# Query loads moved ahead, first load behind mu, and output tiles stored by one DMA

## The chip, the cores and the metric

The kernel runs on one core of a Trainium2 chip. The core has five engines that this document names: PE (TensorE, matrix multiplication), DVE (VectorE), ACT (ScalarE), POOL (GpSimd) and SP (SyncE, which here only issues DMAs). Sixteen DMA engines serve the core. DMAs are issued from SP, ACT or POOL; each of the three has its own queue, and all queues share the sixteen DMA engines. The metric is device time of one execution in microseconds (us), as the median of several executions; lower is better.

## The reference

The computation is an attention through 32 memory slots per head, followed by a gated feed-forward layer. Batch 8, 8 heads, 576 positions, head size 64, so 512 features; the hidden layer has 1024.

```python
def _attn_ref(q, k, v, phi):                      # q, k, v: (8, 8, 576, 64); phi: (8, 8, 576, 32)
    a = softmax(phi over the 576 positions)
    k_m = einsum('bhsm,bhsd->bhmd', a, k)         # 32 memory keys per head
    v_m = einsum('bhsm,bhsd->bhmd', a, v)         # 32 memory values per head
    attn = softmax(q @ k_m^T / sqrt(64))          # 576 x 32 per head
    return attn @ v_m

def _moe_ref(x, mu_k, mu_r, w_k, w_v, w_r):       # x: (8, 576, 512), the heads side by side
    x_prev = x shifted by one position, zeros first
    xk = mu_k * x + (1 - mu_k) * x_prev
    xr = mu_r * x + (1 - mu_r) * x_prev
    k = relu(xk @ w_k)
    v = (k * k) @ w_v
    return sigmoid(xr @ w_r) * v                  # (8, 576, 512), float32
```

## The kernel before

Work goes batch by batch. Of a batch, the exponentials of `phi` (tile `em`) are multiplied with `k` and `v` (tile `kv`) into the memory keys and values (`kvps`), the keys are normalised and transposed (`kbd`, `ktps`, `kmT`), the query is transposed on DVE (`qT`, line 384), the scores (`scps`) are exponentiated on ACT and normalised (`atn`). For batches 1 to 7 the memory values are first multiplied into the weights (`G`), so that the hidden layer (`pk`, `rl`, `sq`) and the gate (`pr`, `sg`) come straight from `atn`. Batch 0 goes the direct way, through the mixed input `x0T`. The output of a tile of 128 positions is `pv` = `sq` times `w_v` on PE, multiplied with the gate into a tile `o` of 128 partitions by 512 float32 on DVE (line 751), and stored from there. There are four buffers of `o`, used in turn: the tile after the next three cannot be written before the stores of this one have landed.

The order is written out by hand. `PLAN` is a list of words that a loop at the end of the function walks through; each word emits the instructions of one step, and every engine executes its instructions in that order. `0:kg0` is a step of batch 0's attention, `c0:7a` a block of the hidden layer, `o:73` an output tile (its first mention emits the matmuls, its second the DVE multiplication and the store), `b:3x8` filler matmuls on zeros that keep PE busy, and `p:...` a load. `p:q:0a` and `p:q:0b` are the two parts of batch 0's query: b the last 4 of 9 column blocks (512 KB read), a the first 5 (640 KB read). Words `0:q1` and `0:q0` transpose these two parts; both write and read one query tile, so program order decides which waits for which.

All loads but the first are issued by POOL's queue, in program order, and convert float32 to bf16 on the way (not `phi`). The list `PRE` is emitted ahead of `PLAN`: the word `id` builds the identity matrix on POOL, `after` is a one-element copy on POOL into `mark` that waits for a load and so holds back what POOL issues behind it. `phi` and `k` of batch 0 are issued on ACT's queue at the very start (lines 169 and 178), and `mu_k` and `mu_r` on SP's queue, 2 KB each (lines 181 and 182): four rows of 128 float32.

Stores are issued by SP (line 728), in the three words of `TAIL` alternately by SP and ACT. An output tile of a batch b > 0 holds four groups of 32 positions; group v goes to rows 18u + 8h' + 2v + r of the output (u from 0 to 31), so a tile is stored by four DMAs of 32 rows:

```python
for v in range(4):
    parts.append((out[b].rearrange("(u x) d -> x u d", u=PB)[8 * h + 2 * v + r], v * PB, PB))
```

Tiles `e0` to `e3` collect what is left of two batches each (two or four parts of 32 rows per tile), and batch 0's tiles consist of parts of 32 or 64 rows, stored in two halves of 256 columns.

Of the kernel before, what the change touches and what calls it, by code (L numbers as in the profile page):

```python
# [17 lines left out]

PLAN = [
# [65 lines left out]

WARM = (10, 8)

PRE = "id: after: q:0b"
TAIL = ("o:70", "o:e3a", "o:e3b",)


NJ = 9
# [5 lines left out]
def kernel(  # L98
# [13 lines left out]
    nc = tc.nc  # L112
# [9 lines left out]
    QR = S // NJ  # L122
    PB = QR // 2
# [34 lines left out]
    mark = const.tile([1, 1], F32, name="mark")  # L158
# [3 lines left out]
    loads = {}  # L162

    def rows(src):
        return src.rearrange("h s d -> (h s) d").rearrange("(a p j) d -> p a (j d)", a=HH, j=NJ)

    def load_phi(b, eng):
        ph = ld.tile([128, HH, NJ, M], F32, name="ph", tag="ph")
        eng.dma_start(out=ph.rearrange("p h j m -> p h (j m)"), in_=rows(phi[b]))
        loads[b] = ph  # L170

    def load_rows(dst, src):
        nc.gpsimd.dma_start(out=dst.rearrange("p h j d -> p h (j d)"), in_=rows(src))
# [6 lines left out]
    mu2 = const.tile([2 * ND, 128], F32, name="mu2")  # L180
# [13 lines left out]
    def preload(word):  # L194

        what, _, part = word.partition(":")
        if what in weights:
            dst, src = weights[what]
            f0, f1 = (int(x) * 128 for x in part.split("-"))
            nc.gpsimd.dma_start(out=dst[:, :, f0:f1], in_=src[:, :, f0:f1])  # L200
        elif what == "id":
            make_identity(nc, identity)
        elif what == "after":
            nc.gpsimd.tensor_copy(mark, loads[0][:1, 0, 0, :1])
        else:
            n = int(part[0])
            if what == "phi":
                load_phi(n, nc.gpsimd)
            else:
                dst = qs[n % 2].rearrange("p (h j) d -> p h j d", j=NJ) if what == "q" else kvs[n % 2][:, "kv".index(what)]  # L210
                src = {"q": q, "k": k, "v": v}[what][n]
                if part[1:] in ("a", "b"):
                    js = HALVES["ab".index(part[1])]
                    js = slice(js.start // QR, js.stop // QR)
                    nc.gpsimd.dma_start(out=dst[:, :, js].rearrange("p h j d -> p h (j d)"),
                                        in_=rows(src)[:, :, js.start * D:js.stop * D])
                elif part[1:] in ("g", "h"):
                    gs = slice(0, 2) if part[1] == "g" else slice(2, 4)
                    nc.gpsimd.dma_start(out=dst[:, gs].rearrange("p h j d -> p h (j d)"), in_=rows(src)[:, gs])
                else:  # L220
                    load_rows(dst, src)

    for word in PRE.split():
        preload(word)
# [12 lines left out]
    for g in range(4):  # L237
        r = slice(g * M, (g + 1) * M)
# [11 lines left out]
    def keep_busy(n, blocks=CT // 64):  # L250
        ps = ps_tile([128, CT], F32, "idle", cover=blocks * 64)[:, :blocks * 64]
        for _ in range(n):
            nc.tensor.matmul(ps.rearrange("p (a b) -> p a b", b=64), lhsT=zeros,  # L253
                             rhs=zeros[:, :64].unsqueeze(1).to_broadcast([128, blocks, 64]), start=True, stop=True,
                             skip_group_check=True)
# [390 lines left out]
    TILES = (0, 128, NP, NP + 128)  # L646
# [56 lines left out]
    queues = [nc.sync]  # L703

    def store(name, o, cols):
        parts = []
        if name[0] == "e":
            for x, b in enumerate((2 * int(name[1]), 2 * int(name[1]) + 1)):
                if b == 0:
                    for r, (j, p) in enumerate(((5, 0), (0, PB))):  # L710
                        parts.append((out[0].rearrange("(p j) d -> j p d", j=NJ)[j, p:p + PB], r * PB, PB))
                else:
                    for r in range(2):
                        parts.append((out[b].rearrange("(u x) d -> x u d", u=PB)[16 + r], x * 64 + r * PB, PB))
        elif name[0] == "0":
            lo = TILES[int(name[1])]
            at = lo
            while at < lo + 128:
                j, p = divmod(at, QR)
                n = min(QR - p, lo + 128 - at)  # L720
                parts.append((out[0].rearrange("(p j) d -> j p d", j=NJ)[(j + 1) % NJ, p:p + n], at - lo, n))
                at += n
        else:
            b, (h, r) = int(name[0]), divmod(int(name[1]), 2)
            for v in range(4):
                parts.append((out[b].rearrange("(u x) d -> x u d", u=PB)[8 * h + 2 * v + r], v * PB, PB))
        for n, (dst, p, rows_) in enumerate(parts):
            queues[n % len(queues)].dma_start(out=dst[:, cols], in_=o[p:p + rows_, cols])

    def value(name, h0=0, h1=1, n=1):  # L730

        def go():
            cols = slice(h0 * Dm // n, h1 * Dm // n)
            pv = ps_tile([128, Dm], F32, "pv", cover=cols.stop - cols.start if n == 1 else 0)
            for fi in range(NF):
                if name[0] == "e":
                    for w in range(4):
                        lo = w * NP + NP - PB
                        nc.tensor.matmul(pv[w * PB:(w + 1) * PB, cols], lhsT=sq[:, fi, lo:lo + PB],  # L739
                                         rhs=wv_sb[:, fi, cols], start=(fi == 0), stop=(fi == NF - 1),  # L740
                                         skip_group_check=True)
                    continue
                lo = int(name[0]) % 2 * S + (TILES[int(name[1])] if name[0] == "0" else
                                             int(name[1]) % 2 * NP + int(name[1]) // 2 * 128)
                nc.tensor.matmul(pv[:, cols], lhsT=sq[:, fi, lo:lo + 128], rhs=wv_sb[:, fi, cols],  # L745
                                 start=(fi == 0), stop=(fi == NF - 1))
            yield
            if name not in outs:
                outs[name] = work.tile([128, Dm], F32, name="o", tag="o", bufs=4)
            o = outs[name]  # L750
            nc.vector.scalar_tensor_tensor(o[:, cols], in0=gated[name][:, cols], scalar=1.0, in1=pv[:, cols],  # L751
                                           op0=AL.add, op1=AL.mult)
            store(name, o, cols)
        return go
# [27 lines left out]
    for word in " ".join(PLAN).split():  # L782
        word, _, used = word.partition("@")
        word, _, now["by"] = word.partition("/")
        now["banks"] = iter(used)
        who, _, name = word.partition(":")
        if who == "p":
            preload(name)
        elif who == "b":
            keep_busy(*map(int, name.split("x")))  # L790
        else:
            queues[1:] = [nc.scalar] * (word in TAIL)
            parts = pending.pop(word, None) or (mixes[who][name] if who in mixes else attend[int(who)](name))()
            if hasattr(parts, "send") and next(parts, who) is not who:
                pending[word] = parts
# [31 lines left out]
```

## Time and profile before

| what | value |
|---|---|
| median of 3 runs | 202.69 us (202.32 to 203.62) |
| the profiled execution | 201.04 us |
| its span, first to last instruction | 198.9 us |
| PE busy | 187.0 us, 94% of the span |
| DVE busy | 157.7 us, 79% |
| ACT busy | 149.3 us, 75% |
| POOL busy | 29.6 us, 15% |
| SP's store DMAs | 146, median 0.42 us each on SP |
| bytes read from and written to HBM | 38.28 MB and 9.44 MB |

Busy time is the share of the span in which an engine executes instructions; DMA issues are not counted. A line of the chain of waits names a start in us, a duration, and the instruction or transfer that the end of the kernel depended on in that stretch. A line of the list of waits gives engine and line, what it waited for, the sum in us, how often, and the longest. In the table of stretches each engine's busy time stands with its number of instructions, followed by the granted clock of PE, the busy share of the sixteen DMA engines (above 1 when packets overlap on an engine) and the GB/s that they wrote.

### The profile page before, as it was taken

What the parts mean: (1) busy time and instruction counts of PE and PEld (TensorE: products, weight loads), DVE (VectorE), ACT (ScalarE), POOL (GpSimd) and SP (SyncE); (2) the same over time, 40 slices, a digit from 0 to 9 for tenths busy, and PEclk for the clock granted to TensorE, in tenths of its full rate; (3) what the DMA queues carried; (4) which work ended last, traced back from release to release, by engine and by line L of the source; (5) the groups of instructions that cost most, each with busy time, mean ns of one, the idle gap of its engine ahead of it and who ended that gap; (6) DMA issues with size and microseconds to landing.
All of it is one profiled execution on the core that took longest, in us unless ns stands there. A gap on an engine that the chain in (4) does not pass through costs nothing.

```text
span 198.9 us, 6428 instructions
## 1 busy us (share of the span) xinstructions
PE 187.0 (94%) x2610; PEld 104.0 (52%) x2610; DVE 157.7 (79%) x348; ACT 149.3 (75%) x352; POOL 29.6 (15%) x45
## 2 busy tenths in 40 slices
PE   8995999799999999999999999999999999999980
PEld 2542475467773466544663566447634574475440
DVE  2232799789987999898999999999799989998230
ACT  2433968699788878877989789987787899887320
POOL 1178242000530120400410211000000000000000
PEclk9999999999999999999999999999999999999998
DMA  5949999999999999896699799944001520043333
GB/s 197 212 57 265 201 209 207 251 218 202 189 206 344 225 260 245 167 246 199 134 238 207 128 232 207 194 98 109 19 15 47 139 69 3 0 117 96 81 84 103
DMA packets 26685, 31.94 MB, mean 161 GB/s; under 512 B 3096, under 2 KB 21280, under 8 KB 26656
## 3 DMA queue, kind: packets, MB, share of 16 engines
q0 software_dynamic: 17888, 20.32, 57.1%
q1 hardware_dynamic: 7408, 9.19, 16.8%
q10 hardware_dynamic: 1360, 2.03, 3.1%
q8 instruction: 20, 0.33, 0.7%
q14 instruction: 9, 0.07, 0.1%
HBM read 38.28 MB, written 9.44 MB: 240 GB/s over the span
## 4 chain that ended last, share of the span: by engine, by line
PE 82%; DMA 7%; DVE 5%; issue 2%; ACT 1%; POOL 0%; DVEq 0%
PE pv L745 27%; PE pk L623 7%; PE pk L615 7%; PE pb L623 7%; PE gps L489 5%; PE pv L739 4%; PE pk L597 4%; PE pr L675 3%; PE pr L667 3%; PE pb L675 3%; PE kvps L318 3%; DMA kv<-in_v_dram 3%; DMA q<-in_q_dram 2%; DMA ph<-in_phi_dram 2%; PE pr L697 2%; PE idle L253 2%
## 5 line engine op out<-in xcount | busy, mean ns | idle before, releaser
L745 PE MATMUL pv<-wv,sq 128*128 128x512 bf16 (+1 forms) x288 | 60.1, 356 | 0.0
L495 ACT CAST G<-gps 128x512 bf16<-128x512 f32 x76 | 40.4, 606 | 4.7 <-PE gps L489 4.4
L745 PEld LDWEIGHTS <-sq 128*128 128x128 bf16 x288 | 27.2, 98 | 27.5 <-issue 3.8
L751 DVE SCALAR_TENSOR_TENSOR o<-sg,pv 128x512 f32<-128x512 f32 (+3 forms) x41 | 24.5, 614 | 9.6 <-PE pv L745 6.4
L623 PEld LDWEIGHTS <-G 128*128 128x128 bf16 x224 | 21.2, 97 | 8.0 <-issue 0.4
L623 PE MATMUL pk<-diff,G 128*128 128x288 bf16 x112 | 22.9, 286 | 0.0
L623 PE MATMUL pb<-diff,G 128*128 128x288 bf16 x112 | 22.9, 286 | 0.0
L589 DVE TENSOR_TENSOR sq<-rl 128x576 bf16<-128x576 bf16 (+2 forms) x51 | 21.0, 426 | 1.0 <-ACT rl L581 0.6
L581 ACT ACTIVATE rl<-pk 128x288 bf16<-128x288 f32 (+2 forms) x42 | 17.2, 422 | 5.7 <-PE pk L597 3.0
L619 ACT COPY pb<-pk 128x288 f32<-128x288 f32 x40 | 15.8, 410 | 6.7 <-PE pk L615 5.6
L615 PE MATMUL pk<-atn,G 128*128 128x288 bf16 x112 | 20.2, 286 | 0.2 <-DVE atn L462 0.2
L253 PE MATMUL idle<-zeros 128*128 128x512 bf16 (+4 forms) x54 | 15.8, 416 | 1.3 <-DVE zeros L179 1.0
L581 ACT ACTIVATE rl<-pb 128x288 bf16<-128x288 f32 x35 | 14.3, 417 | 1.5 <-PE pb L623 0.8
L384 DVE STREAM_TRANSPOSE qT<-q 128x576 uint32<-128x576 uint32 (+2 forms) x16 | 12.1, 765 | 3.7 <-DMA q<-in_q_dram 3.7
L583 DVE TENSOR_SCALAR rl<-pk 128x288 bf16<-128x288 f32 (+2 forms) x30 | 13.3, 454 | 2.0 <-PE pk L597 1.0
L644 ACT ACTIVATE sg<-pb 128x512 f32<-128x512 f32 x14 | 8.5, 610 | 7.7 <-PE pr L697 6.1
L498 DVE TENSOR_TENSOR G<-G 128x1024 bf16<-128x1024 bf16 x21 | 14.1, 684 | 0.0
L615 PEld LDWEIGHTS <-G 128*128 128x128 bf16 x112 | 10.6, 98 | 6.1 <-DVE atn L462 0.4
L644 ACT ACTIVATE sg<-pr 128x512 f32<-128x512 f32 x22 | 13.2, 614 | 0.0
L587 ACT ACTIVATE sq<-rl 128x576 bf16<-128x576 bf16 (+2 forms) x21 | 12.2, 598 | 0.6 <-DVE rl L583 0.3
L462 DVE TENSOR_TENSOR atn<-e,lz 128x576 bf16<-128x576 bf16 (+2 forms) x18 | 11.9, 685 | 0.5 <-ACT lz L434 0.3
L583 DVE TENSOR_SCALAR rl<-pb 128x288 bf16<-128x288 f32 x21 | 9.3, 452 | 1.5 <-PE pb L623 1.4
(99 smaller groups left out, 284.0 us busy)
## 6 DMA issues: line engine op xcount, KB each, us to landing
out_dram<-o SPq DMA_DIRECT2D x134, 64.0 KB, 2.4
ph<-in_phi_dram POOLq DMA_DIRECT2D x7, 576.0 KB, 10.2
kv<-in_v_dram POOLq DMA_DIRECT2D x7, 576.0 KB, 11.4
kv<-in_k_dram POOLq DMA_DIRECT2D x7, 576.0 KB, 10.2
q<-in_q_dram POOLq DMA_DIRECT2D x7, 576.0 KB, 9.4
k0f<-in_k_dram ACTq DMA_DIRECT2D x2, 576.0 KB, 5.7
wv<-in_moe_w_v_dram POOLq DMA_DIRECT2D x2, 512.0 KB, 20.2
ph<-in_phi_dram ACTq DMA_DIRECT2D x1, 576.0 KB, 4.3
```

Of the source, the lines that this page charges most:

```text
L253: nc.tensor.matmul(ps.rearrange("p (a b) -> p a b", b=64), lhsT=zeros, rhs=zeros[:, :64].unsqueeze(1).to_broadcast([128, blocks, 64]), sta ...
L495: return lambda: copier()(g_tile()[:, v, c, GCOLS[i]], st["gps", v, i][c])
L498: return lambda: nc.vector.tensor_sub(g_tile()[:, 1, :, GCOLS[i]], g_tile()[:, 2, :, GCOLS[i]], g_tile()[:, 0, :, GCOLS[i]])
L581: nc.scalar.activation(rl, ps, AF.Relu, scale=HALF ** 0.5)
L583: nc.vector.tensor_scalar(rl, ps, 0.0, HALF ** 0.5, op0=AL.max, op1=AL.mult)
L589: nc.vector.tensor_mul(dst, rl, rl)
L615: nc.tensor.matmul(pa, lhsT=st["G"][:, 2, c, f], rhs=st["at"][:, c, :NP], start=c == 0, stop=False, skip_group_check=True)
L619: copier()(pb, pa)
L623: nc.tensor.matmul(ps, lhsT=st["G"][:, v, c, f], rhs=st["d"][:, kind, c], start=False, stop=c == 1, skip_group_check=True)
L644: nc.scalar.activation(gated[name], ps, AF.Tanh, scale=0.5)
L745: nc.tensor.matmul(pv[:, cols], lhsT=sq[:, fi, lo:lo + 128], rhs=wv_sb[:, fi, cols], start=(fi == 0), stop=(fi == NF - 1))
L751: nc.vector.scalar_tensor_tensor(o[:, cols], in0=gated[name][:, cols], scalar=1.0, in1=pv[:, cols], op0=AL.add, op1=AL.mult)
```

## The change

Four edits. `p:q:0a` moves from behind `0:q1`, the first reader of the query tile, to ahead of it; the lines of `PLAN` are wrapped anew, the other words keep their order. In `PRE`, `after` now stands ahead of `id`, and it waits for `mu_k` in place of `phi`. In `store`, parts that lie in neighbouring partitions become one DMA whose output side has an outer dimension: a tile of 128 positions is stored by one DMA of 4 x 32 rows of 2 KB, the tiles `e0` to `e3` by DMAs of 2 x 32 rows, and where batch 0's tile covers two whole blocks by one DMA of 2 x 64 rows of 1 KB. The other parts of batch 0's tiles stay DMAs of 32 or 64 rows. In the words of `TAIL` the queues still alternate, now from one DMA to the next and over the words.

```diff
-    "0:h0/a 0:h1/a b:3x8@7 b:1x5@7 0:tk@2 0:q1 0:tk b:4x8@7 ...
-    "0:es01 0:mub b:3x8@4 b:1x7@6 0:l01@1 p:q:0a p:v:0g 0:l01 0:vg0@72 0:q0 p:v:0h ...
+    "0:h0/a 0:h1/a b:3x8@7 b:1x5@7 0:tk@2 p:q:0a 0:q1 0:tk b:4x8@7 ...
+    "0:l11 0:es01 0:mub b:3x8@4 b:1x7@6 0:l01@1 p:v:0g 0:l01 0:vg0@72 0:q0 p:v:0h ...
...
-PRE = "id: after: q:0b"
+PRE = "after: id: q:0b"
...
-            nc.gpsimd.tensor_copy(mark, loads[0][:1, 0, 0, :1])
+            nc.gpsimd.tensor_copy(mark, mu2[:1, :1])
...
                 if b == 0:
                     for r, (j, p) in enumerate(((5, 0), (0, PB))):
-                        parts.append((out[0].rearrange("(p j) d -> j p d", j=NJ)[j, p:p + PB], r * PB, PB))
+                        parts.append((out[0].rearrange("(p j) d -> j p d", j=NJ)[j:j + 1, p:p + PB], r * PB, 1))
                 else:
-                    for r in range(2):
-                        parts.append((out[b].rearrange("(u x) d -> x u d", u=PB)[16 + r], x * 64 + r * PB, PB))
+                    parts.append((out[b].rearrange("(u x) d -> x u d", u=PB)[16:18], x * 64, 2))
...
-                parts.append((out[0].rearrange("(p j) d -> j p d", j=NJ)[(j + 1) % NJ, p:p + n], at - lo, n))
+                if n == QR and lo + 128 - at == 2 * QR:
+                    n, j1 = 2 * QR, j + 3
+                    parts.append((out[0].rearrange("(p j) d -> j p d", j=NJ)[j + 1:j1], at - lo, 2))
+                else:
+                    j = (j + 1) % NJ
+                    parts.append((out[0].rearrange("(p j) d -> j p d", j=NJ)[j:j + 1, p:p + n], at - lo, 1))
...
-            for v in range(4):
-                parts.append((out[b].rearrange("(u x) d -> x u d", u=PB)[8 * h + 2 * v + r], v * PB, PB))
-        for n, (dst, p, rows_) in enumerate(parts):
-            queues[n % len(queues)].dma_start(out=dst[:, cols], in_=o[p:p + rows_, cols])
+            parts.append((out[b].rearrange("(u v r) d -> r v u d", u=PB, r=2)[r, 4 * h:4 * h + 4], 0, 4))
+        for dst, p, rows_ in parts:
+            src = o[p:p + rows_ * dst.shape[1], cols]
+            queues[0].dma_start(out=dst[:, :, cols], in_=src)
+            queues.append(queues.pop(0))
...
-            queues[1:] = [nc.scalar] * (word in TAIL)
+            queues[:] = [nc.sync, nc.scalar][:1 + (word in TAIL)] if len(queues) != 1 + (word in TAIL) else queues
```

More of the change, by code (lines that the diff above doesn't have):

```diff
@@ L710, in store @@
                     for r, (j, p) in enumerate(((5, 0), (0, PB))):
-                        parts.append((out[0].rearrange("(p j) d -> j p d", j=NJ)[j, p:p + PB], r * PB, PB))
+                        parts.append((out[0].rearrange("(p j) d -> j p d", j=NJ)[j:j + 1, p:p + PB], r * PB, 1))
                 else:
-                    for r in range(2):
-                        parts.append((out[b].rearrange("(u x) d -> x u d", u=PB)[16 + r], x * 64 + r * PB, PB))
+                    parts.append((out[b].rearrange("(u x) d -> x u d", u=PB)[16:18], x * 64, 2))
         elif name[0] == "0":
-            lo = TILES[int(name[1])]
-            at = lo
+            at = lo = TILES[int(name[1])]
             while at < lo + 128:
```

4 rows, old and new, of the table PLAN are left out of this document.

## The prediction

> **What bounds the kernel now.** I read the busy shares first, then the chain of waits, then the DMA views of the stretches that the change touches.
>
> ```profile
> PE 187.0 (94%) x2610; PEld 104.0 (52%) x2610; DVE 157.7 (79%) x348; ACT 149.3 (75%) x352; POOL 29.6 (15%) x45
> ```
>
> PE is the bound from 20 to 190 us. The start and the end are not PE's. The chain of waits begins so:
>
> ```profile
> 0.74 4.32 DMA ph<-in_phi_dram
> ...
> 5.11 0.12 POOL mark L204
> 5.23 4.91 DMA q<-in_q_dram
> ...
> 10.16 0.72 DVE qT L384
> ...
> 11.18 0.73 POOL q L215
> 11.91 5.48 DMA kv<-in_v_dram
> ...
> 17.43 0.45 PE kvps L318 x36
> ```
>
> The reader is to see a serial start: `phi`, then query part b, then its transpose, which the request for part a waits for, and behind that on POOL's queue the request for `v`. PE stands still from 15.21 to 17.43 us.
>
> At the end the timeline shows SP still issuing stores after the last multiplication:
>
> ```profile
> 193.11 3.65 SPq L728 DMA_DIRECT2D out_dram<-o  x8
> ...
> 193.79 0.35 DVE L751 SCALAR_TENSOR_TENSOR o<-sg,pv 128x192 f32<-128x192 f32 x1 [0.31 <-PE pv L739]
> ```
>
> The last store is issued at 196.34, 2.2 us after DVE ended; the last packet lies between 197.0 and 197.5, the span ends at 198.9.
>
> How wide is a store? The DMA view of 190.5 to 199 us, in which the last 16 stores of 32 rows run, and that of 0 to 1.9 us, in which `mu_k` with its 4 rows lands:
>
> ```profile
> DMA packets 768, 0.79 MB, mean 93 GB/s; under 512 B 256, under 2 KB 512, under 8 KB 768
> ```
> ```profile
> DMA packets 13, 0.01 MB, mean 4 GB/s; under 512 B 4, under 2 KB 13, under 8 KB 13
> ...
> q1 hardware_dynamic: 8, 0.00, 0.4%
> ```
>
> 16 stores carry 512 rows and 256 packets below 512 B: 16 small ones each, one for each DMA engine that takes part. `mu_k` has 4 rows and 4 small ones: a transfer with an outer count of 4 ran on 4 engines. All other transfers here have an outer count of 32, 64 or 128.
>
> **The change part by part.**
>
> *Start.* `mu_k` has landed by 1.9 us, so the copy ends at 2.1, not 5.2. The identity, 0.74 to 1.31 us before, follows and ends near 2.75; DVE's constants behind it (1.34 to 2.64) end near 4.1, before DVE's next work at 6.49: nothing lost. POOL issues b at 2.75 (0.87 us), a at 3.6, the two parts of `v` from 4.4 to 5.8, then `phi` and the weights with no wait. First data follow the issue by some 1.6 us (b: issued 5.23, the pace dips for small rows at 6.8), so from 4.4 us the query shares the DMA engines with `k`, whose second half before was there at 7.92. Up to 0.52 MB of b, and some of a, slip in between; at 0.4 MB per us this delays `k` by 1.3 to 2.9 us, to 9.2 to 10.8. ACT's cast of it (8.23 to 8.89 before) then ends at 9.9 to 11.5. PE took it at 9.85, so up to 1 us is covered by fillers and the rest, 0 to 1.6 us, delays what follows. The transpose now needs a as well (one tile, both writes ahead of it): 2.95 MB at that pace are in by 10.4, against 10.16. In return `v` lands before 15 and the 2.2 us of idle PE go. Ends: gain 2.2 and 0.6; I take 1.8. What is late next is the score chain of part b, which ends at 15.21 already. Later loads run some 3.4 us ahead, the DMA gap from 9.9 to 13.3.
>
> *Stores, issue.* 146 + 6 DMA issues become 55, two of them on ACT. SP idles elsewhere (113 us waiting for DVE). At the end three SP issues remain, the last at 194.2 in place of 196.34: worth 2.0 us if data move as before.
>
> *Stores, width.* A tile is now a DMA of 4 x 32 rows; batch 0's pairs are 2 x 64, `e` tiles 2 x 32. The row of `mu_k` is the only one with such an outer count, and it cannot tell the outer count from the number of rows, which are both 4. The two readings: 16 engines as before, or 4 and 2. I take 4 and 2, the nearest row, and take them to be the same engines each time, which no row shows.
>
> The Trainium skill, page "DMA: Bandwidth & Descriptors", section "Why a DMA increments its semaphore by 16 and not by 1", decides between these readings: the number of engines is the largest up to 16 that divides the slowest dimension of both sides, and from SP or ACT it is the lowest-numbered ones. By it a tile runs on engines 0 to 3 and the sum is the one below; the same page's section "Rules for kernel authors" advises to coalesce many small transfers, and by that alone the sum would be the 3.8 us of gain of the first rival.
>
> Price. At 104 to 109 us only loads run:
>
> ```profile
> 104.00:109.00 5.00, 5.00 (x80) 1.74 (x72) 4.65 (x8) 5.00 (x12) 0.00 (x0) 1.00 1.21 208
> ```
>
> 208 GB/s written as bf16 are 416 read, 26.0 GB/s per engine. A tile on four engines is 65.5 KB each, 2.52 us on these (on sixteen 0.63). Engine 0's queue from the first store to the last tile of batch 3:
> - loads: from 46 us on 12.89 MB are written by POOL's queue, of them 2.95 MB `phi` unconverted, so 22.8 MB read; minus 1.4 MB (3.4 us x 416 GB/s) that are now earlier: 21.4 MB, 1.34 MB per engine.
> - stores: batch 0 four halves of 65.5 KB, four of 8.2, `e0` 74: 369 KB; batches 1 to 3 12 tiles, 786; `e1` 131. Together 1.29 MB.
>
> 2.63 MB at 26.0 GB/s are 101.0 us. The first store is issued at 46.31 - 1.8 = 44.5, its data start 1.3 us later, at 45.8: the queue is through at 146.8. But batch 4's fourth tile, written at 135.2 - 1.8 = 133.4, needs the buffer of batch 3's last one. With four buffers DVE cannot run ahead, so DVE, and behind it PE, stand still for 146.8 + 0.3 - 133.4 = 13.7 us, in pieces, from batch 1 on. Net of the start: 11.9 us late. After that no loads are left, and 2.52 us a tile keep up until the end: the tile issued at 190.83 starts its data at 204.0 and takes until 206.5, the next until 209.0, and `e3` brings 2 x 41 + 2 x 25 = 131 KB onto engine 0: 5.0 us, 214.0, against 197.5 before: 16.6 us late.
>
> **Sum:** -1.8 + 13.7 + 4.7 = +16.6 us; the profiled execution of 201.04 (span 198.9 and 2.1 around it) becomes 217.6. The median of the runs shown is 1.65 us above the profiled execution; I add the change to the median: 219.3 us. The unknown is the rate of one engine: at 25 GB/s it is +21, at 27 +12.5, at 30.1 the stalls are gone. The far end: SP's queue moved 9.19 MB in 16.8% of 16 x 198.9 us, 17.2 GB/s of busy time. With it for the stores the stall is 39 and the tail some 12, 252 us. I keep to 26, because packets overlap (the share is 1.21), so busy time overstates.
>
> **The rivals.**
> 1. *Sixteen engines all the same* (other side). Mechanism: the width follows the 128 rows, not the outer 4. Only the gains are left: 202.69 - 1.8 - 2.0 = 198.9. For it: 4 rows could not use more than 4 engines, so the row of `mu_k` fits as well. It decides if a tile's store shows 16 small packets. The start would have to delay `k` to 11.4 us or more (cast ended at 12.05, 2.2 behind 9.85) to undo its half. Chance 0.14.
> 2. *Four engines, but each store on others.* No engine is overloaded; tail as before: 202.69 - 1.8 = 200.9. Nothing in the trace speaks to it. Chance 0.06.
> 3. *Four engines, no stall before the tail*, since one engine does more than 30.1 GB/s when its neighbours are quiet. Then only the tail: the last full tile's data from 192.6 to 194.8, `e3` 4.4 us, 199.2 against 197.5: 202.69 + 1.7 = 204.4. Against it: no stretch of loads shows over 26. Chance 0.10.
> 4. *The forecast*, four or two and always the same: 0.70, its own range 209 to 230 (rate 27.5 to 24, DVE's 21% of idle time taking some of the stalls).
>
> **How the numbers follow.** Slower by over 1% are cases 4 and 3: 0.80; within 1% (about what a measurement of this kernel can tell from no change) case 2: 0.06; faster case 1: 0.14. Case 4's range holds some 0.66; with cases 3 and 2 it is 0.82, so the range reaches from 200.5 to 230.
>
> **What would show it.** Start: the chain no longer has POOL's request for the query behind DVE; PE's first `v` product near 15.6. Width: in the last stretch few small packets per store, 4 for a tile and 2 for `e3`. Stalls: DVE at its output multiplication waits for `out_dram<-o`, a row that the waits of before lack, with 10 us or more; loads take far longer to land than their 10 us. Tail: last packet over 6 us after DVE's end. Wrong if the tile's stores land in some 2.5 us as before: then the width is 16 or the engines rotate.

## The result and the profile after

| | before | after |
|---|---|---|
| median (lowest to highest) | 203.16 us (202.32 to 203.87), 4 runs | 233.0 us (231.04 to 234.75), 4 runs |
| ratio, 95% interval | 1 | 1.144 (1.133 to 1.154) |
| the profiled execution | 201.04 us | 232.21 us |
| its span | 198.9 us | 230.3 us |

The ratio leaves out the slowest execution of after (234.75 us), which was in a slower state that executions of any kernel here can fall into.

The changed kernel is slower by 31.4 us of span; 16.6 were forecast, and 233.0 lies 3 us above the end of the range. The busy shares of after, one line:

```profile
PE 192.5 (84%) x2610; PEld 105.5 (46%) x2610; DVE 158.4 (69%) x348; ACT 149.4 (65%) x352; POOL 29.6 (13%) x45
```

DVE, ACT and POOL are busy as long as before (157.7, 149.3 and 29.6 us). PE is 5.5 us busier with the same number of matmuls: some of them became slower. The rest of the added time is waiting.

**The start went as the diff promised.** Timeline of after (start, duration, engine, line, operation; in brackets the idle time before it and what ended it):

```profile
2.15 0.18 POOL L204 COPY mark<-mu 1x1 f32<-1x1 f32 x1 [1.70 <-DMA mu<-in_moe_mu_k_dram]
...
8.41 0.77 DVE L303 CAST kv<-k0f 128x576 bf16<-128x576 f32 x1 [1.30 <-DMA k0f<-in_k_dram]
...
11.21 0.71 DVE L384 STREAM_TRANSPOSE qT<-q 128x512 uint32<-128x512 uint32 x1 [1.38 <-DMA q<-in_q_dram]
...
15.00 0.45 PE L318 MATMUL kvps<-kv,em 64*32 64x64 bf16 x36
```

The mark comes at 2.15 in place of 5.11, PE's first product with `v` at 15.00 in place of 17.43. The first output multiplication comes at 43.62, where it was at 45.87. DVE's cast of the second half of `k`, which waits for the load, begins at 8.41; in the timeline of before it is

```profile
7.92 0.46 DVE L303 CAST kv<-k0f 128x576 bf16<-128x576 f32 x1 [0.97 <-DMA k0f<-in_k_dram]
```

so with the early query traffic `k` was there 0.5 us later.

**A tile's store is four engines wide.** DMA view of after in a stretch with stores alone, 156 to 164 us, with the packets by size and the share of sixteen engines by queue:

```profile
DMA packets 354, 0.70 MB, mean 88 GB/s; under 512 B 10, under 2 KB 10, under 8 KB 354
...
q1 hardware_dynamic: 354, 0.70, 25.1%
```

344 rows of 2 KB are 2.7 tiles of 128, and they come with 10 small packets: nearly 4 a tile, where a tile of before brought 4 x 16. A share of 25.1% of sixteen engines is four engines busy all the time, and 0.70 MB in 8 us are 88 GB/s: **22 GB/s per engine**.

**The stalls.** List of waits of after (engine, line, what it waited for: us in all, times, longest). In the kernel that has only the start edits (first experiment) the first row is missing and the second is one wait of 1.7 us:

```profile
DVE o L755 <- DMA out_dram<-o: 13.4, 5, 8.2
...
DVE qT L384 <- DMA q<-in_q_dram: 7.9, 2, 6.5
```

The chain of waits of after has three long pieces of transfer (start, duration):

```profile
59.41 22.81 DMA out_dram<-o
...
108.25 14.50 DMA q<-in_q_dram
...
135.30 22.85 DMA out_dram<-o
```

A store is on its way for some 22 us, and a load of a query for 14.5. Issue to landing of a query is 16.2 us in the median, before 9.4. The first piece is not a store of four engines: DVE's wait of 8.16 us that it ends, the longest, is for the buffer of batch 0's last tile, whose second half is stored as 2 x 64 rows of 1 KB on two engines. From 65 to 70 us, beside loads, 72 such rows are stored, 7.4 GB/s on each of the two; from 50 to 52 us, alone, 62 rows, 16 GB/s. The third piece covers two waits of DVE. Where the waits end, in the timeline of after:

```profile
82.31 0.69 DVE L755 SCALAR_TENSOR_TENSOR o<-sg,pv 128x512 f32<-128x512 f32 x1 [8.16 <-DMA out_dram<-o]
...
122.78 0.78 DVE L384 STREAM_TRANSPOSE qT<-q 128x576 uint32<-128x576 uint32 x1 [6.50 <-DMA q<-in_q_dram]
...
150.87 0.69 DVE L755 SCALAR_TENSOR_TENSOR o<-sg,pv 128x512 f32<-128x512 f32 x1 [3.07 <-DMA out_dram<-o]
...
158.17 0.69 DVE L755 SCALAR_TENSOR_TENSOR o<-sg,pv 128x512 f32<-128x512 f32 x1 [1.23 <-DMA out_dram<-o]
```

The last of these is batch 4's fourth tile, from which the prediction read its stall: forecast for about 147.1, it came at 158.17.

**Behind each long stall PE runs at half clock.** Table of stretches of after (stretch, length, busy us and instructions of PE, PE's weight loads, DVE, ACT, POOL, then the granted clock, DMA share, GB/s): the long stall, then the stretch behind each of the stalls that end at 82.31, 122.78 and 150.87:

```profile
71.00:82.00 11.00, 1.82 (x11) 0.89 (x10) 1.98 (x3) 2.37 (x5) 0.00 (x0) 0.79 0.75 147
82.50:87.50 5.00, 3.71 (x20) 1.84 (x20) 4.31 (x11) 1.83 (x4) 0.00 (x0) 0.50 0.25 85
126.00:129.00 3.00, 3.00 (x92) 1.64 (x77) 2.97 (x4) 1.71 (x5) 0.83 (x2) 0.56 0.22 40
152.50:156.00 3.50, 3.50 (x11) 1.37 (x9) 3.19 (x8) 0.69 (x2) 0.00 (x0) 0.51 0.27 94
```

PE's busy time times the clock that is missing: 3.71 x 0.50 + 3.00 x 0.44 + 3.50 x 0.49 = 4.9 us. The clock of before has no such stretch.

**The tail.** End of the timeline of after; the first line is SP's queue, issuing the last full tiles and half of `e3`, the second the last two multiplications:

```profile
208.12 8.66 SPq L731 DMA_DIRECT2D out_dram<-o  x6
...
214.95 0.96 DVE L755 SCALAR_TENSOR_TENSOR o<-sg,pv 128x320 f32<-128x320 f32 x2 [0.85 <-PE pv L743]
```

DVE ends at 215.91, the last data packet at 228.83: 12.9 us, where before had 194.14 and 197.51, 3.4.

**The account**, against the kernel with the start edits alone (span 196.1; DVE's end 191.23): waits for stores 13.4 + wait for the query 6.5 + half clock 4.9 = 24.8, and DVE ends 215.91 - 191.23 = 24.7 later. To before: -2.8 (start) + 24.8 + 9.5 (tail, 12.9 - 3.4) = +31.5, and 31.4 were measured. The terms overlap a little: 0.5 of the 24.7 was there at the first output multiplication already (43.62 against 43.09), before any store.

### The profile page after: what moved, and what is told of

The parts are those of the page before. It is cut to its first block, busy times and chain, and to the rows that moved or that the text cites. A ratio compares the mean times of both kernels' runs of the same rounds, so it can differ in the third digit from the quotient of the medians.

```text
span 230.3 us, 6296 instructions
## 1 busy us (share of the span) xinstructions
PE 192.5 (84%) x2610; PEld 105.5 (46%) x2610; DVE 158.4 (69%) x348; ACT 149.4 (65%) x352; POOL 29.6 (13%) x45
## 4 chain that ended last, share of the span: by engine, by line
PE 57%; DMA 26%; DVE 7%; issue 2%; ACT 1%; POOL 0%; SPq 0%; DVEq 0%
DMA out_dram<-o 20%; PE pv L749 17%; PE idle L253 7%; DMA q<-in_q_dram 6%; PE pk L615 4%; PE pk L623 4%; PE pb L623 4%; PE gps L489 3%; PE pk L597 3%; PE kvps L318 3%; PE pr L675 2%; PE pb L675 2%; PE pv L743 2%; PE pr L667 1%; PE pr L697 1%
## 5 line engine op out<-in xcount | busy, mean ns | idle before, releaser
L749 PE MATMUL pv<-wv,sq 128*128 128x512 bf16 (+1 forms) x288 | 62.1, 364 | 0.0
L755 DVE SCALAR_TENSOR_TENSOR o<-sg,pv 128x512 f32<-128x512 f32 (+3 forms) x41 | 24.7, 613 | 25.4 <-DMA out_dram<-o 13.4
L749 PEld LDWEIGHTS <-sq 128*128 128x128 bf16 x288 | 27.7, 100 | 28.9 <-issue 6.0
L615 PE MATMUL pk<-atn,G 128*128 128x288 bf16 x112 | 20.7, 290 | 12.3 <-DVE rl L583 10.2
L384 DVE STREAM_TRANSPOSE qT<-q 128x576 uint32<-128x576 uint32 (+2 forms) x16 | 12.1, 764 | 7.9 <-DMA q<-in_q_dram 7.9
L489 PEld LDWEIGHTS <-vT 64*32 64x32 bf16 x336 | 4.2, 89 | 16.4 <-issue 15.4
L412 ACT ACTIVATE e<-scps 128x288 bf16<-128x288 f32 x28 | 9.2, 417 | 1.6 <-PE scps L398 1.6
## 6 DMA issues: line engine op xcount, KB each, us to landing
q<-in_q_dram POOLq DMA_DIRECT2D x7, 576.0 KB, 16.2
```

Of the source, the lines that this page charges most:

```text
L615: nc.tensor.matmul(pa, lhsT=st["G"][:, 2, c, f], rhs=st["at"][:, c, :NP], start=c == 0, stop=False, skip_group_check=True)
```

## The experiments

Medians stand against the kernel before on the same chip. No kernel leaves out part of the computation.

**1. The start alone, and the stores alone.** First the changed kernel with the whole of `store` and its queues as before:

```diff
-            parts.append((out[b].rearrange("(u v r) d -> r v u d", u=PB, r=2)[r, 4 * h:4 * h + 4], 0, 4))
+            for v in range(4):
+                parts.append((out[b].rearrange("(u x) d -> x u d", u=PB)[8 * h + 2 * v + r], v * PB, PB))
...
-            queues[:] = [nc.sync, nc.scalar][:1 + (word in TAIL)] if len(queues) != 1 + (word in TAIL) else queues
+            queues[1:] = [nc.scalar] * (word in TAIL)
```

> The start edits alone (the query's part a requested ahead of the first reader, POOL's first load behind mu_k), every store as before. Theory N (the loss is the width of the stores: 4 or 2 DMA engines, always the same ones, at some 21 GB/s each while storing): only the start is left, 2.2 us as the changed kernel's first output multiplication shows it (43.62 against 45.87 us), so 203.2 - 2.2 = 201.0 us. Rival S (the earlier loads are what collides, with k or with each other, and the stores only suffer from it): no gain, 203 us or more, and late landings of k and of the loads behind.

Measured: 199.5 us against 202.47, ratio 0.986 (0.980 to 0.993), span 196.1. Its last multiplication, in the timeline:

```profile
190.88 0.35 DVE L751 SCALAR_TENSOR_TENSOR o<-sg,pv 128x192 f32<-128x192 f32 x1 [0.31 <-PE pv L739]
```

193.79 before: DVE ends 2.9 us earlier, and the span 2.8. The start is a gain, a little larger than forecast.

Then the other half, the kernel before with the whole of the new `store` and its queues:

```diff
-            for v in range(4):
-                parts.append((out[b].rearrange("(u x) d -> x u d", u=PB)[8 * h + 2 * v + r], v * PB, PB))
+            parts.append((out[b].rearrange("(u v r) d -> r v u d", u=PB, r=2)[r, 4 * h:4 * h + 4], 0, 4))
```

> The stores alone as in the changed kernel, the start as before. Theory N: the whole loss and a little more, since loads are 3.4 us later when the first store comes: 233 + 2.2 + about 2 = 237 us. Rival S: clearly less than the changed kernel, 205 to 215 us.

Measured: 234.29 us, ratio 1.156 (1.148 to 1.165). The list of waits has the same two rows as after:

```profile
DVE o L755 <- DMA out_dram<-o: 15.0, 5, 8.2
DVE qT L384 <- DMA q<-in_q_dram: 8.1, 3, 4.2
```

All of the loss comes from the stores.

**2. Two DMAs of 2 x 32 rows per tile.** This halves the outer count and doubles the DMAs. If the number of DMAs or their descriptors were the matter, or if each store went to other engines, this would not be worse than after; if the outer count is the width and the engines are always the same, two engines carry all.

```diff
-            parts.append((out[b].rearrange("(u v r) d -> r v u d", u=PB, r=2)[r, 4 * h:4 * h + 4], 0, 4))
+            for v in (0, 2):
+                parts.append((out[b].rearrange("(u v r) d -> r v u d", u=PB, r=2)[r, 4 * h + v:4 * h + v + 2], v * PB, 2))
```

> The changed kernel, but each full tile of batches 1 to 7 as two DMAs of 2 x 32 rows in place of one of 4 x 32. Theory N: the width is the outer count and both DMAs lie on the same two engines, so a tile puts 131 KB in place of 65.5 KB on each of them: through batch 3 (1.34 MB of loads at 26 and 2.07 MB of stores at 21 GB/s) 150 us from 45.4, then 2.36 MB more at 21 GB/s, 112 us: about 310 us; two small packets per store. Rival R (narrow, but each DMA on other engines, and the loss is the long landing of one large DMA): a smaller DMA lands sooner, no slower than 233 us. Rival W (16 engines all the same, the loss comes from the size of the DMA or its issue): between 203 and 233 us, 16 small packets per store.

Measured: 282.37 us (one run). DMA view of 210 to 240 us, where stores are alone:

```profile
DMA packets 732, 1.50 MB, mean 50 GB/s; under 512 B 23, under 2 KB 23, under 8 KB 729
...
q1 hardware_dynamic: 729, 1.45, 13.0%
```

and its list of waits:

```profile
DVE o L756 <- DMA out_dram<-o: 71.3, 15, 9.9
```

13.0% of sixteen is 2.1 engines, with 2 small packets per 64 rows; 1.45 MB in 30 us are 48 GB/s, 24 per engine. Four buffers let up to eight of these DMAs be outstanding, DVE waits for them again and again, and still only two engines work: they are the same two. (A queue that takes up one DMA after the other would leave two engines busy as well, whichever they are. Against that, in every half microsecond from 76.5 to 81.5 us of after the trace has rows of 1 KB and rows of 2 KB, which belong to different stores of SP's queue.) The loss is some 28 us smaller than expected; two engines did a little more each than four.

**3. Where in the kernel the narrow stores cost.** Both kernels have the start edits, with the new store (`store_narrow`) for some tiles alone and that of before (`store_wide`) for the others. First only for batches 6 and 7 and `e3`, in whose time few loads are left:

```diff
+    def store(name, o, cols):
+        (store_narrow if name in ('60', '61', '62', '63', '70', '71', '72', '73', 'e3') else store_wide)(name, o, cols)
```

> The start edits, and the one-DMA stores only for the tiles of batches 6 and 7 and the last e tile; all loads have landed by then. Theory N: a tile takes 65.5 KB at 21 GB/s, 3.1 us, on its engines. Batch 6's four start at 173.4 and are through at 185.9, then 73 to 71 until 198.3, then 131 KB of the e tile until 204.5, against 197.5 before: 203.2 + 7.0 = 210 us, with no wait of DVE for a store. Had the rate been the 26 GB/s of the loads: 203.2 - 2.2 + 4.7 = 205.7 us. Rival W (wide all the same): 203.2 - 2.2 - 1.9 = 199.1 us.

Measured: 208.6 us, ratio 1.020 (1.013 to 1.027). No wait of DVE for a store; DVE ends at 191.27, as in the kernel with the start alone (191.23), and the last data come at 203.68 in place of 194.59. So the **tail by itself costs 9.1 us**. DMA view of 174 to 184 us of this kernel:

```profile
DMA packets 428, 0.87 MB, mean 87 GB/s; under 512 B 11, under 2 KB 11, under 8 KB 426
...
q1 hardware_dynamic: 426, 0.85, 25.0%
```

The four engines are busy throughout at 0.85 MB / 10 us / 4 = 21 GB/s, and from 174 us on they cannot catch up. This is a mean of slow and quick passages: from 176 to 184 us alone it is 0.79 MB, 24.7 GB/s per engine.

Then only for the 12 full tiles of batches 1 to 3, where loads run. This one tells two readings of the stall apart. A count of all the work on one engine up to batch 4, as the prediction made it, gives no stall here, since batch 0's and the `e` tiles are spread over sixteen: 1.34 MB of loads, 0.79 of narrow stores and 0.10 of the others at 26 GB/s are 85.5 us, which end at 131.3, ahead of 133.4. A loss that arises wherever a narrow store shares its engines with loads is there all the same.

```diff
+        (store_narrow if name in ('10', '11', '12', '13', '20', '21', '22', '23', '30', '31', '32', '33') else store_wide)(name, o, cols)
```

> The start edits, and the one-DMA stores only for the 12 full tiles of batches 1 to 3, while loads run. Theory C (the loss in the middle is one engine's total work, as the forecast counted it): 0.79 MB of stores and 1.34 MB of loads on engine 0 are 83 us at 25 to 26 GB/s, from about 68 us (first narrow store) with most loads after it, so through before 133 us: no stall, the time of the start edits alone, 0.986 of before, 199.6 us. Theory L (the loss is local: a store that shares its engines with loads gets a third to a half of them, so a bunch of tiles waits for its buffers or holds up a load that is needed soon, whatever the total): waits of DVE for stores or for a query load in this stretch, 203 to 210 us.

Measured: 211.28 us against 201.81, ratio 1.049 (1.042 to 1.057); span 210.5, 14.4 over the start alone. Two of its four waits, in the timeline:

```profile
97.66 0.69 DVE L783 SCALAR_TENSOR_TENSOR o<-sg,pv 128x512 f32<-128x512 f32 x1 [3.71 <-DMA out_dram<-o]
...
125.83 0.69 DVE L783 SCALAR_TENSOR_TENSOR o<-sg,pv 128x512 f32<-128x512 f32 x1 [5.00 <-DMA out_dram<-o]
```

and the stretches behind these, columns as above:

```profile
98.00:102.00 4.00, 3.60 (x13) 1.83 (x13) 4.00 (x10) 1.70 (x4) 0.15 (x1) 0.57 1.02 278
126.00:133.00 7.00, 5.84 (x23) 3.12 (x23) 5.45 (x13) 1.81 (x5) 1.48 (x2) 0.53 0.68 137
```

The four waits are 9.7 us; half clock takes 3.60 x 0.43 + 5.84 x 0.47 = 4.3 (the start alone has clock 1.00 in both stretches): together 14.0. But 2.3 of the 14.4 were there before any narrow store: the first output multiplication came at 45.41, in the start alone at 43.09. (From 6 to 9 us PE did 10 matmuls in this execution and 53 in that one, with the same instructions; why is not shown.) So the narrow stores cost 12.1, and some 2 us of the 14.0 did not lengthen the kernel. The count as the prediction made it does not hold here. With 22 GB/s for the stores it would leave 45.8 + 51.5 + 40.2 + 0.3 - 133.4 = 4.4 us, under half of the 9.7.

**4. More buffers.** If the stalls come from a store that is long on its way, and not only from engines that are full, more buffers must take them away. The changed kernel with eight `o` buffers:

```diff
-        ... name="o", tag="o", bufs=4
+        ... name="o", tag="o", bufs=8
```

> The changed kernel with 8 buffers of o in place of 4. If the stalls come through the output buffers (DVE waiting for out_dram<-o, 13.4 us, and what these push into the loads), they go and the time falls by 10 to 20 us, to 213 to 223 us; the tail stays, and may grow to some 10 us, since the stores are then further behind. If it is rather the loads held up on the crowded engines (DVE waiting for the query, 6.5 us at 116 us), DVE's waits for stores go but its waits for loads grow, and the time stays above 225 us.

Measured: 218.77 and 223.67 us; the second had its first output multiplication at 47.46, 3.8 us later than after, before any store. Its list of waits:

```profile
DVE qT L384 <- DMA q<-in_q_dram: 6.1, 1, 6.1
DVE o L755 <- DMA out_dram<-o: 3.9, 1, 3.9
```

The waits for stores fall from 13.4 to 3.9 and the wait for the query stays: buffers hide the stores, not the delayed loads. The same eight buffers in the kernel of batches 1 to 3:

> The narrow stores for batches 1 to 3 alone, with 8 buffers of o. Theory B (their 12 us come in through DVE's waits for a buffer, 9.7 us, and PE's half clock after each, some 4 us): both go, and the time is that of the start edits, 199 to 201 us. Rival H (the loads held up on the crowded engines cost as much): waits of DVE for a query load appear and the time stays at 205 us or more.

Measured: 202.12 and 205.23 us, where four buffers gave 211.28. No wait for a store is left. In the timeline and the table of stretches of the second:

```profile
108.78 0.78 DVE L384 STREAM_TRANSPOSE qT<-q 128x576 uint32<-128x576 uint32 x1 [3.65 <-DMA q<-in_q_dram]
```
```profile
112.00:116.00 4.00, 4.00 (x95) 1.97 (x80) 3.93 (x8) 3.27 (x9) 1.48 (x2) 0.57 0.46 85
```

3.65 us of waiting and 4.00 x 0.43 = 1.7 of half clock are 5.4. The span is 203.5, against 196.3 of the start alone on the same chip (below); of these 7.2 us 2.6 were there at the first output multiplication (45.85 against 43.26), which leaves 4.6. The other execution is 202.12 - 198.43 = 3.7 above the median of the start alone. So about 4 of the 12 us stay, more than if only the buffers counted. The narrow stores do harm in two ways: the tile's buffer comes free late, and loads that the same engines carry land late.

**5. What in the start gains.** The request order alone: the kernel of the start edits, with the mark behind the identity and on `phi` as before:

```diff
-PRE = "after: id: q:0b"
+PRE = "id: after: q:0b"
...
-            nc.gpsimd.tensor_copy(mark, mu2[:1, :1])
+            nc.gpsimd.tensor_copy(mark, loads[0][:1, 0, 0, :1])
```

> Only the query's part a is requested earlier; POOL's first load waits for phi as before, behind the identity; stores as before. Part b is then issued at 5.2, a at 6.1, v from 6.9 us; v's first half is there at about 12, before the score chain of part b ends at 15.2. Theory Q (the gain of the start is the order of the requests alone): the same as with both start edits, ratio 0.986. Rival M (the earlier mark brings part of it): ratio 0.990 or more, v's first product on PE clearly later than 15.0 us.

Measured: 200.1 us against 201.81, ratio 0.993 (0.989 to 0.997). And the mark alone, in the kernel before:

```diff
-PRE = "id: after: q:0b"
+PRE = "after: id: q:0b"
...
-            nc.gpsimd.tensor_copy(mark, loads[0][:1, 0, 0, :1])
+            nc.gpsimd.tensor_copy(mark, mu2[:1, :1])
```

> Only POOL's first load behind mu_k and the mark ahead of the identity; the query's part a is requested behind the first reader as before, all stores as before. Part b then lands before 9 us, its transpose ends some 1 us earlier than 10.87, so part a is requested 1 to 1.5 us earlier and v with it; PE's first v product at about 16.2 in place of 17.43. Theory Q (the order of the requests is what counts): half of the gain, ratio 0.993. Rival M (the mark brings most): ratio 0.988 or less.

Measured: 202.0 us against 202.69, ratio 0.994 (0.990 to 0.999). Both together, the kernel of the start edits unchanged, once more on the chip of the last:

> Both start edits, all stores as before, once more with more rounds beside the other two: ratio 0.986 as before. If the gain of 2.2 to 2.9 us that the start shows on PE is all that changes, 0.986 to 0.989.

Measured: 198.43 us against 202.69, ratio 0.982 (0.977 to 0.987). PE's first product with `v` in the three timelines, mark on `phi`, mark alone, both:

```profile
15.23 0.45 PE L318 MATMUL kvps<-kv,em 64*32 64x64 bf16 x36
```
```profile
10.47 0.74 POOL L215 DMA_DIRECT2D q<-in_q_dram  x1 [6.75 <-DVE qT L384]
...
16.52 0.45 PE L318 MATMUL kvps<-kv,em 64*32 64x64 bf16 x36 [1.79 <-DMA kv<-in_v_dram]
```
```profile
14.56 0.45 PE L318 MATMUL kvps<-kv,em 64*32 64x64 bf16 x36
```

With the mark alone POOL still stands behind DVE's transpose for 6.75 us, and `v` still ends 1.79 us of idle PE. The request order gains 2.2 us of that moment (17.43 to 15.23), the mark 0.9, both 2.9. Executions differ by nearly as much as the mark brings: in after, which has both, this product is at 15.00. With the request order alone the first output multiplication comes at 43.80, with both at 43.26. With the mark alone it comes at 46.48 (before 45.87), but that execution had PE at a granted clock of 0.51 from 17.5 to 21 us, so this says nothing about the mark. The two ratios multiply to 0.987, the end of the whole's interval, so how the 1.8% divide is not settled.

**6. Is there more to have at the end?** With the old stores SP still issues 32-row DMAs when the last tiles are done. The start edits, with `o:71` added to the words that alternate with ACT:

```diff
-TAIL = ("o:70", "o:e3a", "o:e3b",)
+TAIL = ("o:70", "o:71", "o:e3a", "o:e3b",)
```

> The start edits with all stores as before, and o:71 added to TAIL, so that the last full tile's four stores go alternately to SP and ACT. SP then issues 6 DMAs after 190 us in place of 8; the last one starts about 1.1 us earlier. Theory I (the end is bound by SP's issues of 0.42 to 0.46 us each): 199.5 - 1.0 = 198.5 us, ratio to before 0.981. Rival D (the end is bound by the transfers and the fixed time behind the last store): no change, ratio 0.986.

Measured: 199.11 us against 201.81, ratio 0.988 (0.983 to 0.994): no better than the start alone (0.986 and 0.982). The timeline (of an execution of 202.38 us, longer than most of this kernel, so only the order is read from it) has ACT's gate behind ACT's own two stores, which wait for DVE:

```profile
194.05 0.85 ACTq L728 DMA_DIRECT2D out_dram<-o  x2
194.95 0.60 ACT L644 ACTIVATE sg<-pr 128x512 f32<-128x512 f32 x1 [1.65 <-DVE o L751]
```

The same with POOL, which is idle there:

```diff
-            queues[1:] = [nc.scalar] * (word in TAIL)
+            queues[1:] = [nc.gpsimd] if word == "o:71" else [nc.scalar] * (word in TAIL)
```

> Both start edits, stores as before, but o:71's four go alternately to SP and POOL, which is idle at the end, so that ACT's gate activations wait for none of them. Theory I (SP's issues bind the end): SP's last issue 0.9 us earlier, ratio 0.982. Rival D (fixed time behind the last store, or POOL's slower issue takes the place): no change to both start edits alone, 0.986 or more.

Measured: 198.17 us against 202.69, ratio 0.982 (0.976 to 0.988); last data at 193.62, against 194.59 with the start alone of the first experiment. In time it cannot be told from the start alone on its chip (198.43). These two are the best versions seen, 1.8% faster than the kernel before.

## Why the prediction was wrong in size, step by step

- **Direction and mechanism: right.** Slower, because a DMA of 4 x 32 rows runs on four engines and always the same. The small packets per tile (4) and per 64 rows (2), and the shares of 25.1% and 13.0%, show the width; two-by-two with its 282 us, and stores of two sizes side by side, exclude engines that change. This is what the Trainium skill, page "DMA: Bandwidth & Descriptors", section "Why a DMA increments its semaphore by 16 and not by 1", gives for SP's queue, and the trace agrees in the count (4.0 and 2.1 engines busy); that they are the lowest-numbered ones no run here shows. By the line of the Trainium skill's section "Rules for kernel authors" (same page) to coalesce small transfers alone, the kernel should have gained; it lost 14%. The line of the same table of the Trainium skill that an outermost dimension below 16 confines a DMA to at most that many engines is the one that decides here, and the trace agrees (4.0 engines).
- **Start, "I take 1.8": undersized.** 2.8 us in the spans. The failing piece is the delay of `k` by 1.3 to 2.9 us from sharing; it came 0.5 us later. The top end was 2.2: the first output multiplication moved by 45.87 - 43.62 = 2.25 in after and by 2.8 in the start alone. What the start gains beyond 2.2 is not explained.
- **"Stores, issue: worth 2.0 us": not seen,** as the sum had it, because the engines' backlog and not SP ends the kernel.
- **"The rate of one engine, 26.0 GB/s": too high.** It was read from loads. Stores alone run at 21 to 25 GB/s per engine, by stretch, in rows of 2 KB, and at 16 in batch 0's rows of 1 KB. Beside loads they get less: from 114 to 121 us of after both kinds run,

```profile
q0 software_dynamic: 1120, 1.29, 107.1%
q1 hardware_dynamic: 122, 0.24, 10.1%
```

  and the four engines pass 0.24 MB / 7 us / 4 = 8.6 GB/s each of stores. That is the sharing and not a slower transfer: 10.1% of sixteen is 40% of four engines, so in the time that they spend on stores they move 21 GB/s, as alone.
- **"Engine 0's total work", stall 13.7: the failing step.** Waits for stores came to 13.4 in total, by coincidence near the 13.7: the largest, 8.2, is for a buffer of batch 0, stored at 7.4 GB/s per engine where the sum had 26. And the term holds more than the waits: DVE is 24.7 later at the end than with the start alone, and batch 4's fourth tile +23.0 where +11.9 stood. With 22 GB/s for the stores the same formula gives the queue's end 1.34 MB / 26 + 1.29 MB / 22 = 110.2 us after 45.8, and the tile 21 late, close to it; but for the kernel of batches 1 to 3 it gives under half of the waits that were measured, so it is at most a part of the mechanism. A narrow store is slow wherever it meets loads, and two terms were missing: loads that share its engines are late themselves (the query, 6.5 us), and each stall is followed by half clock (4.9 us).
- **Tail, "+4.7": half of it.** 9.5 in after, 9.1 alone. The step "2.52 us a tile keep up until the end" failed: at 22 GB/s a tile takes 65.5 KB / 22 = 3.0 us, and the four engines are busy without a pause (25.0% of sixteen, 174 to 184 us of the tail's own kernel). Eight tiles and `e3` put 655 KB on one engine; at 22 instead of 26 GB/s that is 4.6 us more, which is what was missing.
- **Sum:** forecast -1.8 + 13.7 + 4.7 = 16.6; measured -2.8 + 24.8 + 9.5 = 31.5. "At 25 GB/s it is +21" pointed the right way: the range stopped at a rate of 24, and 22 was outside it.
- **Open:** why the rate of stores alone varies from 21 to 25 GB/s, and how an engine divides its time between the two queues. From 78 to 82 us of after few loads are left:

```profile
q1 hardware_dynamic: 108, 0.16, 15.4%
q0 software_dynamic: 58, 0.06, 9.3%
```

  In each half microsecond of these, up to 81.5, the trace has 7 load packets and 7 or 8 rows of 1 KB of batch 0's store, as if its two engines took a packet of each queue in turn; the trace does not name a packet's engine, so this is not shown. A one-DMA store with an outer count of 16 or more would need another assignment of positions to partitions; it wasn't tried.

## What to carry to other kernels

Before stores are merged into fewer DMAs, read how many engines one of them uses: count the small packets (under 512 B) per transfer where it is alone, and multiply the queue's share by sixteen. A merged store whose outer count is 4 is four engines wide, and the price is not the issue time that was saved but the longer way of each store: buffers come free late, loads on the same engines land late, and PE pays again in half clock behind each stall. Size such a term with the rate of the same kind of transfer in the same company, not with that of loads that run alone.

## What was not expected of the hardware

- One DMA engine stored at 21 to 25 GB/s (SBUF to HBM, rows of 2 KB) where it loaded at 26, at 16 in rows of 1 KB, and at 8.6 (rows of 2 KB) with loads beside it, which left it 40% of its time.
- A stall in which DVE, and PE behind it, waited 3 to 8 us was followed by 3 to 7 us at a mean granted clock of 0.50 to 0.57. The Trainium skill, page "TensorE: Matmul & The Clock Gate", section "Part 1: The HAM clock gate (the "warmup" mystery)", has about 3.4 us at half rate until the clock comes back; the trace agrees, with 3.5 us at 0.51 (152.5 to 156 us). The stretches of 5 and 7 us are longer, and PE was idle in parts of these.
- Part b of the query was requested 2.4 us earlier (2.84 in place of 5.23) and part a right behind it, 1.18 MB beside the second half of `k`, and `k` came only 0.5 us later.
